# Values as two scaled f16 parts instead of three bf16 parts in the attention product of a fused attention and MLP kernel

## The chip, the cores and the metric

The kernel runs on 1 core of one Trainium2 chip. The metric is device microseconds of one execution, the median of several runs. Three runs of the kernel before gave 973.56, 976.33 and 977.08 us; the median is 976.33 us.

## The reference

Causal attention with a learned decay over 4 batches of 8 heads, 576 positions, head dimension 64, all in float32; then two MLPs with a squared ReLU, 2304 tokens, 512 features, 2048 hidden units.

```
scores = q @ k.T / 8 + (cum[i] - cum[j])     # cum = cumsum(log f), causal mask
attn   = softmax(scores)                     # rows
x      = attn @ v                            # (4, 8, 576, 64) -> (2304, 512)
h      = max(x @ w_in, 0);  x = (h * h) @ w_out
h      = max(x @ w_in2, 0); out = (h * h) @ w_out2
```

## The kernel before, in words

Every float32 product is taken apart into products of shorter parts, so that TensorE runs each at one pass. Nothing is issued in the order of the source: each piece of work is an `op` with an engine, an assumed duration, a priority, the ops it depends on and the buffers it uses. `Plan.run` walks a model of time over them and emits the instructions of every engine in the order it finds. That order is fixed in the program; on the chip each engine takes its instructions in order and waits on semaphores. When an op's assumed duration or its place among the buffers changes, the order of all engines changes with it.

The first 64 queries of every head (`first_part`) and the next 128 (`pair`) are done at the start, while the first MLP's weights are loaded, decoded and split. The remaining 384 queries of each head are a `unit(b, h)`: 32 units, eight to a batch. The first MLP (`mlp_a`, groups g = 0 to 8 of 256 tokens, products at L861 and L936, 12 matmuls to a block, 32 blocks to a group) fills TensorE between them. Group 3 needs all units of batch 0, group 4 those of batches 0 and 1. The second MLP (L1233, L1259) follows; its weights are prepared when the last unit is done.

A unit has these steps. SP loads q and k (`raw`, L652); ACT, DVE and POOL split them (L659 to L674). TensorE computes the scores in four pieces, two matmuls each (L713), into two banks `bk`. DVE takes the row maximum (L409), ACT the exponential (L417), DVE the reciprocal (L423, L426). ACT writes the high f16 part of the probabilities (`p_hi`, L432) and DVE the low one (`p_lo`, L439) into `ph`. SP issues a transposing DMA of `ph` into `pt` (L731). There is one `pt` buffer (`npt=1`), so the transpose of a unit is issued when the product of the unit before has read it. Then TensorE multiplies `pt` with the values (`av`, L750), and ACT (L766) and DVE (L768) add the upper and lower 64 rows of the result into `X` with the constant factor 2^-15.

The values of a head are loaded (L697) into every other row of 64 of a buffer `vv`, of which there are two. `v_parts` makes two subtractions on POOL (L448): the float32 numbers' upper halves serve as bf16 parts in place. In `av` the stationary operand of ten matmuls is 128 wide (high and middle part of the values beside each other), once for the high and once for the low part of the probabilities. Five more matmuls have the third part of the values, 64 wide, each put into one half of the output rows, as the table `THIRD` says.

Of the kernel before, what the change touches and what calls it, by code (L numbers as in the profile page):

```python
# [7 lines left out]
F32 = mybir.dt.float32  # L8
# [17 lines left out]
THIRD = ((0, 0), (1, 1), (3, 0), (2, 1), (4, 0))  # L26
# [39 lines left out]
class Op:  # L66
    __slots__ = ("how", "prio", "uses", "nwait", "ready", "outs", "data", "turn", "dmas", "rows")


class Plan:  # L70
# [17 lines left out]
    def op(self, eng, dur, fn, prio, deps=(), uses=(), data=None, other=None, dmas=1, rows=128):  # L88
# [3 lines left out]
        o.how, o.uses, o.data, o.dmas, o.rows, o.turn = {eng: (dur, fn, 0)}, tuple(uses), data, dmas, rows, dur == self.TURN[0]  # L92
# [13 lines left out]
    def run(self):  # L106
# [15 lines left out]
        while todo:  # L122
            again = True
            while again:
                again = False
                for e in engs:
# [66 lines left out]
                    if o.data is not None and e == "SP":  # L193
                        free[e] = t
                        _, a, z = self.TURN if o.turn else self.COPY
                        for _ in range(o.dmas):
# [4 lines left out]
                            end = lanes[issued % 8] = dma + self.LAT["DMA"] + (self.TURNED if o.turn else 0.0)  # L201
# [61 lines left out]
def attention_then_two_squared_relu_mlps(  # L263
# [111 lines left out]
    stat = ap_.tile([128, 2, 3, 8], F32, name="stat")  # L375
    PP = Pool([(x, stat[:, i, 0], stat[:, i, 1], stat[:, i, 2])
# [6 lines left out]
    ident = pair_p.tile([128, 128], F32, name="ident")  # L383
# [59 lines left out]
    def v_parts(vv, n, prio, dep):  # L443


        def rest(eng, i):
            x = vv()[:, :, i]
            eng.tensor_tensor(out=vv()[:, :, 1] if i == 0 else x.bitcast(BF16)[:, :, 0::2], in0=x,  # L448
                              in1=x.bitcast(BF16)[:, :, 1::2], op=ALU.subtract)

        for i in range(2):
            dep = either(TUNE["vr"], ("POOL", pool_(n * D), lambda i=i: rest(nc.gpsimd, i)),
                         ("DVE", dvs(n * D), lambda i=i: rest(nc.vector, i)), prio, [dep], [vv_of[vv]])
        return dep

    vv_of = {}
# [186 lines left out]
    def unit(b, h, prio, first):  # L643
# [5 lines left out]
        vv_of[vv] = vv  # L649
# [46 lines left out]
        def load_v():  # L696
            nc.sync.dma_start(out=vv()[:, :, 0], in_=v[b, h])  # L697

        ov = op("SP", P.COPY[0], load_v, prio + TUNE["vd"], [ld], [vv], data=0.91)
        ov = v_parts(vv, 5, prio + TUNE["vd"], ov)  # L700
# [35 lines left out]
        def av():  # L736
            x, w_, z = pT(), vv().bitcast(BF16), o()
# [787 lines left out]
```

## Time and profile before

| | |
|---|---|
| median of 3 runs | 976.33 us |
| the profiled execution | 977.94 us |
| its span, first to last instruction | 976.2 us |
| mean granted TensorE clock | 0.982 |
| TensorE busy | 948.3 us, 97% |
| VectorE (DVE), ScalarE (ACT), GpSimd (POOL) busy | 683.6, 453.1, 361.4 us |

The program is one core's, so there is one row of busy times. A busy TensorE at 97% says that whatever leaves its stream shortens the span, unless a wait takes its place; which waits are near is read stage by stage. The units lie between 131 us (first scores) and 484 us (last `av`).

### The profile page before, as it was taken

The page shows a single profiled execution, that of the slowest core. Times are in us where ns is not written, and L with a number is a line of the kernel's source. Part 1 is how long each engine was busy: PE and PEld are TensorE (multiplying, and loading weights), DVE is VectorE, ACT ScalarE, POOL GpSimd, SP SyncE. Part 2 cuts the span into 40 slices and gives each one's busy share as a digit, 9 for nine tenths or more (in the row PEclk, how much of TensorE's full clock was granted, in tenths as well). Part 3 has the DMA queues.
Part 4 walks back from the last instruction along what each step waited for, and adds up shares of the span by engine and source line. Part 5 has one row for each costly group of instructions (what it writes and reads, how often), then busy time and mean ns, then how long its engine had stood idle before and what let it go on. Part 6 is the DMA issues. An engine that isn't in the chain of part 4 may idle for free.

```text
span 976.2 us, 17134 instructions
## 1 busy us (share of the span) xinstructions
PE 948.3 (97%) x6463; PEld 866.7 (89%) x6463; DVE 683.6 (70%) x1341; ACT 453.1 (46%) x900; POOL 361.4 (37%) x315
## 2 busy tenths in 40 slices
PE   6999999999999999999999999999999999999997
PEld 3888898999997999999999998988898988989886
DVE  7998667787768778876478689888874445734343
ACT  3686677777777678775333353223230112311011
POOL 2244443444434435434232435332351314522130
PEclk7799999999999999999999999999999999999999
DMA  8767245666656756755546524674452111322113
GB/s 251 253 202 207 83 104 119 140 129 146 132 110 134 148 122 134 143 118 120 120 160 207 173 82 157 199 242 159 134 171 88 64 65 65 117 86 79 65 65 108
DMA packets 177187, 131.91 MB, mean 135 GB/s; under 512 B 140944, under 2 KB 155536, under 8 KB 175056
## 3 DMA queue, kind: packets, MB, share of 16 engines
q1 hardware_dynamic: 176848, 130.32, 49.1%
q8 instruction: 51, 0.84, 0.4%
q10 hardware_dynamic: 256, 0.49, 0.2%
q14 instruction: 32, 0.26, 0.1%
HBM read 85.07 MB, written 18.42 MB: 106 GB/s over the span
## 4 chain that ended last, share of the span: by engine, by line
PE 70%; DVE 11%; issue 9%; POOL 3%; ACT 3%; DMA 2%; POOLq 0%; SPq 0%; ACTq 0%; DVEq 0%
PE yp L936 16%; PE hp L861 16%; PE hp L1233 13%; PE bk L1259 10%; PE bk L750 5%; PE yp L1259 5%; PE bk L713 4%; POOL g L1246 2%; DVE ph L439 1%; DVE tmp L818 1%; DVE tmp L820 1%; DVE pp L409 1%; DVE w L1122 1%; POOL gt L886 1%; DVE w L837 1%
## 5 line engine op out<-in xcount | busy, mean ns | idle before, releaser
L936 PE MATMUL yp<-gt,w 128*128 128x256 f32 x1728 | 231.6, 283 | 1.8 <-POOL gt L886 1.7
L861 PE MATMUL hp<-xk,w 128*128 128x256 f32 x1728 | 227.7, 282 | 1.1 <-DVE w L837 0.8
L936 PEld LDWEIGHTS yp<-gt,w 128*128 128x128 f32 x1728 | 216.5, 189 | 6.2 <-POOL gt L886 3.1
L861 PEld LDWEIGHTS hp<-xk,w 128*128 128x128 f32 x1728 | 215.3, 190 | 3.0 <-DVE w L837 1.0
L886 POOL TENSOR_TENSOR gt<-sq,gt 128x512 fp32r<-128x512 f32 x72 | 97.3, 1352 | 154.4 <-ACT gt L883 135.9
L1259 PE MATMUL bk<-w,g 128*128 128x512 f32 x576 | 148.5, 394 | 0.7 <-POOL g L1246 0.7
L1246 POOL TENSOR_TENSOR g<-r,g 128x768 fp32r<-128x768 f32 x36 | 66.8, 1855 | 203.2 <-ACT g L1245 199.3
L1233 PE MATMUL hp<-w 128*128 128x384 f32 x630 | 123.9, 335 | 0.1
L1259 PEld LDWEIGHTS bk<-w,g 128*128 128x128 f32 x576 | 106.6, 188 | 18.7 <-POOL g L1246 1.6
L1245 ACT CAST g<-r 128x768 fp32r<-128x768 f32 x47 | 39.3, 835 | 180.1 <-DVE r L1244 180.0
L1233 PEld LDWEIGHTS hp<-w 128*128 128x128 f32 x630 | 111.7, 188 | 8.1 <-DVE st L1210 0.4
L417 ACT ACTIVATE pp<-pp,stat 128x448 f32<-128x448 f32 (+1 forms) x128 | 78.4, 613 | 44.6 <-DVE stat L409 37.0
L439 DVE SCALAR_TENSOR_TENSOR ph<-pp,stat,ph 128x320 f16<-128x320 f32 (+2 forms) x96 | 77.3, 814 | 15.5 <-ACT ph L432 13.9
L1210 DVE TENSOR_TENSOR r<-hp,st 128x384 f32<-128x384 f32 x62 | 34.5, 556 | 62.8 <-PE hp L1233 62.7
L448 POOL TENSOR_TENSOR vv<-vv 128x320 f32<-128x320 f32 x64 | 54.4, 850 | 54.8 <-DMA vv<-in_v_dram 42.1
L1244 DVE SCALAR_TENSOR_TENSOR r<-r 128x768 f32<-128x768 f32 x47 | 73.6, 1567 | 1.4
L1259 PE MATMUL yp<-w,g 128*128 128x512 f32 x288 | 74.5, 393 | 0.0
L1233 PE MATMUL hp<-w,far 128*128 128x384 f32 x378 | 74.1, 335 | 0.0
L870 ACT ACTIVATE sq<-hp 128x512 f32<-128x512 f32 x72 | 42.8, 594 | 66.8 <-PE hp L861 66.3
L1233 PEld LDWEIGHTS hp<-w,far 128*128 128x128 f32 x378 | 67.3, 188 | 4.7
L409 DVE CUSTOM_DVE_ANT_0 pp<-bk,mask 128x448 f32<-128x448 f32 (+1 forms) x128 | 59.4, 476 | 15.3 <-PE bk L713 9.9
L873 DVE SCALAR_TENSOR_TENSOR sq<-hp,sq 128x512 f32<-128x512 f32 x64 | 44.0, 688 | 35.1 <-ACT sq L870 34.7
(171 smaller groups left out, 1281.5 us busy)
## 6 DMA issues: line engine op xcount, KB each, us to landing
w<-wo_d SPq DMA_DIRECT2D x48, 512.0 KB
stage<-in_w_dram SPq DMA_DIRECT2D x26, 512.0 KB
raw<-in_qk_dram SPq DMA_DIRECT2D x32, 288.0 KB
wo_d<-part SPq DMA_DIRECT2D x16, 512.0 KB
ph<-in_w_dram SPq DMA_DIRECT2D x7, 1024.0 KB
st<-in_w_dram SPq DMA_DIRECT2D x6, 1024.0 KB
vv<-in_v_dram SPq DMA_DIRECT2D x32, 160.0 KB
qk_a<-in_qk_dram SPq DMA_DIRECT2D x16, 192.0 KB
```

Source lines behind the costliest of these rows:

```text
L409: nc.vector.tensor_tensor_reduce(out=x[:rows, c0:c0 + wd], in0=src, in1=msk, scale=-0.125, scalar=3.0e38 if first else nmax[:rows, 5:6], o ...
L417: nc.scalar.activation(out=x, in_=x, func=AF.Exp, scale=-1.0, bias=nmax[:rows, t:t + 1], accum_out=ssum[:rows, t:t + 1])
L439: nc.vector.scalar_tensor_tensor(out=flat[:rows, z:z + wd], in0=x, scalar=r, in1=flat[:rows, 128 * blk:128 * blk + wd], op0=ALU.mult, op1= ...
L448: eng.tensor_tensor(out=vv()[:, :, 1] if i == 0 else x.bitcast(BF16)[:, :, 0::2], in0=x, in1=x.bitcast(BF16)[:, :, 1::2], op=ALU.subtract)
L750: nc.tensor.matmul(dst.rearrange("p (n c) -> p n c", n=rh.shape[1]), lhsT=lt, rhs=rh, start=(i == 0), stop=(i == len(todo) - 1), skip_grou ...
L861: nc.tensor.matmul(ps, lhsT=lt, rhs=rh, start=(k_ == 0 and c == 0), stop=(k_ == KD - 1 and c == 2))
L886: eng.tensor_tensor(out=gt[1]()[:, :c], in0=sq()[:, :c], in1=f32(gt[0]()[:, :c]), op=ALU.subtract)
L936: nc.tensor.matmul(yp[d // 2]()[:, d % 2], lhsT=lt, rhs=rh, start=(i == 0 and c == 0 and d % 2 == 0), stop=(i == NF - 1 and c == 2), skip_ ...
L1233: nc.tensor.matmul(ps()[:, 0:TH], lhsT=lt, rhs=rh, start=(k_ == 0 and c == 0), stop=(k_ == 1 and c == 2))
L1244: o = op("DVE", dvs(TU), lambda r=r: nc.vector.scalar_tensor_tensor(out=r(), in0=r(), scalar=0.0, in1=r(), op0=ALU.max, op1=ALU.mult), e0, ...
L1246: l = either_vp(TU, lambda e, r=r, g=g: e.tensor_tensor(out=g()[:, 1], in0=r(), in1=f32(g()[:, 0]), op=ALU.subtract), e0, [h], [r, g])
L1259: nc.tensor.matmul(bank(ob[c]), lhsT=g()[:, a, c * 128:(c + 1) * 128], rhs=rw()[:, b], start=(p == 0 and x == 0 and z == 0), stop=(p == NP ...
```

## The change

The values of a head are scaled by a power of two, so that they fit f16, and split into two f16 parts: the high part by ACT (scaled copy), the low part by DVE (times the scale, minus the high part). The five 64-wide matmuls of `av` and the two subtractions on POOL are gone, and the values are loaded as one run of 320 numbers per partition. The fold takes the inverse scale from a table `up_down` instead of the constant.

The scale is one number for each head, from the largest absolute value of the head. A new function `scales(b)` loads all values of a batch once more, 2560 numbers per partition in pieces, heads spread over 16 partitions each; DVE reduces each piece to a maximum per partition. A float32 matmul with these maxima as a stationary operand and the identity as the moving one lays them along the columns of all 128 partitions; six small DVE instructions make the two factors for eight heads. For batch 0 the pieces (1024, 1024, 512) go into parts of `X` not yet in use, for the others five pieces of 512 go through the two halves of `st`. The third piece onward waits for the reduction of the piece two before.

```diff
-    def v_parts(vv, n, prio, dep):
-        def rest(eng, i):
-            x = vv()[:, :, i]
-            eng.tensor_tensor(out=vv()[:, :, 1] if i == 0 else x.bitcast(BF16)[:, :, 0::2], in0=x,
-                              in1=x.bitcast(BF16)[:, :, 1::2], op=ALU.subtract)
-        for i in range(2):
-            dep = either(TUNE["vr"], ("POOL", pool_(n * D), lambda i=i: rest(nc.gpsimd, i)),
-                         ("DVE", dvs(n * D), lambda i=i: rest(nc.vector, i)), prio, [dep], [vv_of[vv]])
+    def v_parts(vv, b, h, prio, dep):
+        up = up_down[:, b, 0, h:h + 1]
...
+        def hi():
+            nc.scalar.activation(out=parts_v(vv)[:, :, 0], in_=x(), func=AF.Copy, scale=up)
+        def lo():
+            nc.vector.scalar_tensor_tensor(out=parts_v(vv)[:, :, 1], in0=x(), scalar=up, in1=parts_v(vv)[:, :, 0], op0=ALU.mult, op1=ALU.subtract)
+        o = op("ACT", act(5 * D) + 0.09, hi, prio, [dep, scale_of[b]], [vv])
+        return op("DVE", dvs(5 * D) + 0.08, lo, prio, [o], [vv])
+    def scales(b, prio, pieces, deps):
+        src = v[b].rearrange("h (y q) n d -> (h y) (q n d)", y=128 // H)
...
+            o = op("SP", P.COPY[0], load, prio, deps + [os_[j - 2] if j > 1 else None], data=n * 0.00143, lag=2.0)
+            os_.append(op("DVE", dve(n), top_of, prio, [o]))
...
+        o = op("DVE", 0.08, lambda: nc.vector.tensor_reduce(out=top[:, 7:8], in_=top[:, 0:k], op=ALU.max, axis=mybir.AxisListType.X), prio, os_)
+        ps = Buf(BK)
+        def spread():
+            nc.tensor.matmul(ps()[:, 0:128], lhsT=top[:, 7:8].to_broadcast([128, 128]), rhs=ident, start=True, stop=True, skip_group_check=True)
+        o = op("PE", mm4(128), spread, prio, [o, o_m2], [ps])
...
+        for y in range(6):
+            o = op("DVE", 0.2 if y == 0 else 0.08, lambda y=y: step(y), prio, [o], [ps] if y == 0 else [])
+        scale_of[b] = o
...
-                    todo.append((z[:, q], w_[:, j].rearrange("p z d -> p (z d)")[:, 1::2], x[:, n.start + z0:n.stop + z0:n.step]))
-            for i, half in THIRD:
-                j, q, n = cuts[i]
-                todo.append((z[64 * half:64 * half + 64, q], w_[:, j, 1, 0::2], x[:, n]))
+                    todo.append((z[:, q], w_[:, j].rearrange("p z d -> p (z d)"), x[:, n.start + z0:n.stop + z0:n.step]))
...
-        o_av = op("PE", 1.65, av, prio, [o_tr, ov] + gone, [pT, vv, o])
+        o_av = op("PE", 1.35, av, prio, [o_tr, ov] + gone, [pT, vv, o])
...
+        scales(0, TUNE["BP0"] - 40.0, early, [decoded[14]] + aug_second)
+        scales(1, 3850.0, later, w_all + [all_att[-8]])
+        scales(2, 5350.0, later, w_all + [all_att[-8]])
+        scales(3, 6850.0, later, w_all + [all_att[-8]])
```

The change moves the order on every engine. In the changed program the lines below `v_parts` are higher by 55 to 61: scores are L771, `av` L805, the MLP products L916 and L991, the transpose L789, loads of q and k L710, of values L755 (of `scales` L479), the spread matmul L494, the high and low part of the values L458 and L461.

On TensorE, the end of the product of unit 15 (counted from 1), before, and what follows it; `64x384` and the like are the third parts:

```order
L750 LDWEIGHTS vv_103
L750 MATMUL bk_89<-pt_101,vv_103 128x128
L750 LDWEIGHTS vv_103
L750 MATMUL bk_89<-pt_101,vv_103 64x384
L750 LDWEIGHTS vv_103
L750 MATMUL bk_89<-pt_101,vv_103 64x384
L750 LDWEIGHTS vv_103
L750 MATMUL bk_89<-pt_101,vv_103 64x256
L750 LDWEIGHTS vv_103
L750 MATMUL bk_89<-pt_101,vv_103 64x384
L750 LDWEIGHTS vv_103
L750 MATMUL bk_89<-pt_101,vv_103 64x128
```

And the end of the same product now:

```order
L805 LDWEIGHTS vv_103
L805 MATMUL bk_89<-pt_101,vv_103 128x256
L805 LDWEIGHTS vv_103
L805 MATMUL bk_89<-pt_101,vv_103 128x128
L805 LDWEIGHTS vv_103
L805 MATMUL bk_89<-pt_101,vv_103 128x128
L991 MATMUL yp_93<-gt_81,w 128x256
```

The ten wide matmuls stay, the five narrow ones are gone, and an MLP block follows directly.

On TensorE, what stands between the products of units 15 and 16 before; in all there are three MLP blocks, and the eight score matmuls (L713) stand together:

```order
L861 MATMUL hp_92<-xk_83,w 128x256 x6
L713 MATMUL bk_87<-qk_1231 128x320
L713 MATMUL bk_87<-qk_1229 128x320
L713 MATMUL bk_88<-qk_1231 128x448
L713 MATMUL bk_88<-qk_1229 128x448
L713 MATMUL bk_87<-qk_1231 128x288
L713 MATMUL bk_87<-qk_1229 128x288
L713 MATMUL bk_88<-qk_1231 128x288
L713 MATMUL bk_88<-qk_1229 128x288
L936 MATMUL yp_94<-gt_81,w 128x256
```

And the same place now:

```order
L771 MATMUL bk_88<-qk_1237 128x320
L771 MATMUL bk_88<-qk_1235 128x320
L771 MATMUL bk_87<-qk_1237 128x448
L771 MATMUL bk_87<-qk_1235 128x448
L991 MATMUL yp_93<-gt_79,w 128x256
L991 MATMUL yp_93<-gt_80,w 128x256
L991 MATMUL yp_93<-gt_79,w 128x256 x2
L991 MATMUL yp_93<-gt_80,w 128x256
L991 MATMUL yp_93<-gt_79,w 128x256
L991 MATMUL yp_94<-gt_79,w 128x256
L991 MATMUL yp_94<-gt_80,w 128x256
L991 MATMUL yp_94<-gt_79,w 128x256 x2
```

An MLP block now follows the first four score matmuls, and there are five blocks between these two units. Between units 16 and 17 there are four now. Between most others there are five, as before.

On SP, the stretch from the transpose of unit 3 to that of unit 5 before (`pt<-ph` is a transpose, `raw` a load of q and k):

```order
L731 DMA_TRANSPOSE pt_101<-ph 128x26x128
L697 DMA vv_104<-in_v_dram 128x5x64
L652 DMA raw<-in_qk_dram 128x576
L731 DMA_TRANSPOSE pt_101<-ph 128x26x128
L697 DMA vv_103<-in_v_dram 128x5x64
L652 DMA raw<-in_qk_dram 128x576
L957 DMA y_d<-st 128x2x128 x4
L731 DMA_TRANSPOSE pt_101<-ph 128x26x128
```

And now:

```order
L789 DMA_TRANSPOSE pt_101<-ph 128x26x128
L755 DMA vv_104<-in_v_dram 128x320
L710 DMA raw<-in_qk_dram 128x576
L479 DMA st<-in_v_dram 128x512 x2
L789 DMA_TRANSPOSE pt_101<-ph 128x26x128
L755 DMA vv_103<-in_v_dram 128x320
L710 DMA raw<-in_qk_dram 128x576
L479 DMA st<-in_v_dram 128x512
L789 DMA_TRANSPOSE pt_101<-ph 128x26x128
L1012 DMA y_d<-st 128x2x128 x4
```

Loads of `scales` for the next batch (L479) now stand before two transposes in a row, and before the one ahead of them, too; the third to fifth of them wait for a reduction on DVE.

## Rows read from the trace of the kernel before

**Rows 1.** The page's first part: busy time, share and instructions of each engine.

```profile
PE 948.3 (97%) x6463; PEld 866.7 (89%) x6463; DVE 683.6 (70%) x1341; ACT 453.1 (46%) x900; POOL 361.4 (37%) x315
```

**Rows 2.** Windows: stretch, busy PE, PEld, DVE, ACT, POOL, then granted clock, DMA.

```profile
200.00:250.00 50.00, 49.72 (x401) 45.35 (x400) 37.99 (x109) 36.55 (x76) 19.38 (x20) 1.00 0.62 133
250.00:300.00 50.00, 49.55 (x401) 45.98 (x400) 36.61 (x104) 36.19 (x74) 20.96 (x21) 1.00 0.64 131
...
500.00:550.00 50.00, 50.00 (x425) 49.81 (x424) 39.53 (x53) 14.72 (x25) 17.11 (x13) 1.00 0.71 230
```

**Rows 3.** Timeline of TensorE, one `av` product, from its first, ninth, tenth, eleventh matmul.

```profile
181.92 1.93 PE L750 MATMUL bk<-pt,vv 128*128 128x384 f16 x15
...
183.12 0.56 PE L750 MATMUL bk<-pt,vv 128*128 128x128 f16 x4
...
183.18 0.50 PE L750 MATMUL bk<-pt,vv 128*128 128x128 f16 x3
...
183.33 0.52 PE L750 MATMUL bk<-pt,vv 128*64 128x384 f16 x5
183.78 0.40 PE L713 MATMUL bk<-qk 128*128 128x288 f32 x1
```

**Rows 4.** Timeline of TensorE from the end of one product to the next.

```profile
195.36 0.80 PE L713 MATMUL bk<-qk 128*128 128x288 f32 x4
...
202.36 1.53 PE L936 MATMUL yp<-gt,w 128*128 128x256 f32 x12
203.73 1.93 PE L750 MATMUL bk<-pt,vv 128*128 128x384 f16 x15
```

**Rows 5.** Lines by form, whole span: busy, mean ns, idle before, releasers.

```profile
L439 DVE SCALAR_TENSOR_TENSOR ph<-pp,stat,ph 128x320 f16<-128x320 f32 x32 | 24.3, 759 | 3.1 <-ACT ph L432 1.8
L432 ACT ACTIVATE ph<-pp,stat 128x320 f16<-128x320 f32 x32 | 17.7, 554 | 2.5 <-DMA pt<-ph 1.1 <-DVE stat L426 0.7 <-DVE stat L423 0.5
L448 POOL TENSOR_TENSOR vv<-vv 128x320 bf16<-128x320 f32 x32 | 28.9, 903 | 1.9
L448 POOL TENSOR_TENSOR vv<-vv 128x320 f32<-128x320 f32 x32 | 25.5, 796 | 53.0 <-DMA vv<-in_v_dram 42.1 <-PE bk L713 10.0 <-PE hp L861 0.7
L495 DVE TENSOR_REDUCE tmp<-tmp 128x8 f32<-128x512 f32 x2 | 1.4, 677 | 0.0
L426 DVE RECIPROCAL stat<-stat 128x1 f32<-128x1 f32 (+1 forms) x112 | 18.0, 161 | 2.7
```

**Rows 6.** Source L439: minimum, median, maximum ns, first and last start.

```profile
L439 DVE SCALAR_TENSOR_TENSOR ph<-pp,stat,ph x96: 534/789/1527, 134.3 to 471.7; 128x320 f16<-128x320 f32 x32, 128x448 f16<-128x448 f32 x32, 128x576 f16<-128x576 f32 x32
```

**Rows 7.** Timeline of TensorE, float32 transposes with the identity and what follows.

```profile
97.65 0.79 PE L615 MATMUL bk<-ident,pp 128*128 128x128 f32 x3 [0.53 <-ACT pp L605]
98.27 0.94 PE L589 MATMUL bk<-qk_a 66*128 66x192 f32 x6
```

**Rows 8.** Timeline of TensorE at units 15 and 16, and windows of the same stretch.

```profile
305.64 0.87 PE L713 MATMUL bk<-qk 128*128 128x320 f32 x4
307.92 1.08 PE L713 MATMUL bk<-qk 128*128 128x288 f32 x4 [1.41 <-DVE stat L409]
...
309.58 2.18 PE L936 MATMUL yp<-gt,w 128*128 128x256 f32 x11 [0.46 <-POOL gt L886]
311.56 2.96 PE L750 MATMUL bk<-pt,vv 128*128 128x384 f16 x15
314.46 1.68 PE L936 MATMUL yp<-gt,w 128*128 128x256 f32 x12
...
310.00:315.00 5.00, 5.00 (x29) 3.54 (x28) 4.09 (x9) 1.98 (x5) 2.69 (x3) 0.66 0.21 59
```

**Rows 9.** Timeline of SP: the transpose ahead of the product at 203.73.

```profile
195.47 4.01 SPq L731 DMA_TRANSPOSE pt<-ph  x1
```

**Rows 10.** Windows of the stretch in which batch 0's scales fall.

```profile
110.00:120.00 10.00, 9.08 (x73) 8.48 (x72) 3.56 (x4) 4.37 (x9) 5.97 (x12) 1.00 0.01 2
```

More of the change, by code (lines that the diff above doesn't have):

```diff
@@ L200, in run @@
                             dma = max(dma, dge + z) + o.data / o.dmas
-                            end = lanes[issued % 8] = dma + self.LAT["DMA"] + (self.TURNED if o.turn else 0.0)
+                            end = lanes[issued % 8] = dma + self.LAT["DMA"] + (self.TURNED if o.turn else 0.0) + o.lag
                             issued += 1
@@ L375, in attention_then_two_squared_relu_mlps @@
     stat = ap_.tile([128, 2, 3, 8], F32, name="stat")
+    top = ap_.tile([128, 8], F32, name="top")
+    ident = ap_.tile([128, 128], F32, name="ident")
+    up_down = ap_.tile([128, B, 2, H], F32, name="up_down")
     PP = Pool([(x, stat[:, i, 0], stat[:, i, 1], stat[:, i, 2])
@@ new lines, in attention_then_two_squared_relu_mlps, with load, top_of, step @@
+    scale_of = {}
+    def scales(b, prio, pieces, deps):
+        src = v[b].rearrange("h (y q) n d -> (h y) (q n d)", y=128 // H)
+        c, os_, last = 0, [], [None] * len(pieces)
+        for j, x in enumerate(pieces):
+            n = 1
+            for y in x.shape[1:]:
+                n *= y
+            def load(x=x, c=c, n=n):
+                s_ = src[:, c:c + n]
+                nc.sync.dma_start(out=x, in_=s_.rearrange("p (a c) -> p a c", a=x.shape[1]) if len(x.shape) == 3 else s_)
+            def top_of(x=x, j=j):
+                nc.vector.tensor_reduce(out=top[:, j:j + 1], in_=x, op=ALU.max, axis=mybir.AxisListType.XY if len(x.shape) == 3 else mybir.AxisListType.X,
+                                        apply_absolute_value=True)
+            o = op("SP", P.COPY[0], load, prio, deps + [os_[j - 2] if j > 1 else None], data=n * 0.00143, lag=2.0)
+            os_.append(op("DVE", dve(n), top_of, prio, [o]))
+            c += n
+        assert c == src.shape[1]
+        k = len(pieces)
+        o = op("DVE", 0.08, lambda: nc.vector.tensor_reduce(out=top[:, 7:8], in_=top[:, 0:k], op=ALU.max, axis=mybir.AxisListType.X), prio, os_)
[3 more added lines that the diff above has]
+        o = op("PE", mm4(128), spread, prio, [o, o_m2], [ps])
+        m, up, down = up_down[:, b, 1], up_down[:, b, 0].bitcast(U32), up_down[:, b, 1].bitcast(U32)
+        def step(y):
+            if y == 0:
+                nc.vector.tensor_reduce(out=m, in_=ps()[:, 0:128].rearrange("p (h y) -> p h y", h=H), op=ALU.max, axis=mybir.AxisListType.X)
+            elif y == 1:
+                nc.vector.tensor_scalar(out=m, in0=m, scalar1=1.0e-27, scalar2=None, op0=ALU.max)
+            elif y == 2:
+                nc.vector.tensor_scalar(out=down, in0=down, scalar1=0x7F800000, scalar2=None, op0=ALU.bitwise_and)
+            elif y == 3:
+                nc.vector.tensor_scalar(out=up, in0=down, scalar1=0x7F800000, scalar2=None, op0=ALU.bitwise_xor)
+            elif y == 4:
+                nc.vector.tensor_scalar(out=up_down[:, b, 0], in0=up_down[:, b, 0], scalar1=2.0 ** 13, scalar2=None, op0=ALU.mult)
+            else:
+                nc.vector.tensor_scalar(out=m, in0=m, scalar1=2.0 ** -29, scalar2=None, op0=ALU.mult)
+        for y in range(6):
+            o = op("DVE", 0.2 if y == 0 else 0.08, lambda y=y: step(y), prio, [o], [ps] if y == 0 else [])
+        scale_of[b] = o
@@ L736, in av @@
         def av():
[L737 removed]
+            x, w_, z = pT(), parts_v(vv), o()
             cuts = []
@@ L1423, in attention_then_two_squared_relu_mlps @@
         opened = op("POOL", 0.01, open_qk, TUNE["BP0"] - 1.0, a_tr + [o_ph])
+        early = [X[:, :, 768:1024], X[:, :, 0:256], X[:, 0:2, 768:1024]]
+        later = [st_[j % 2][:, 512:1024] for j in range(5)]
+        scales(0, TUNE["BP0"] - 40.0, early, [decoded[14]] + aug_second)
         for h in range(H):
```

25 lines of the change are left out of this document (13 added, 12 removed).

## The prediction

> **What bounds the kernel now.** I read the busy times first: TensorE is busy for 97% of the span [rows 1], so the time is what stands in its stream plus its waits. Then the windows by stage: through the units TensorE is busy for 49.7 and 49.6 of 50 us, and after the last unit for 50.00 of 50 [rows 2]. DVE (38.0 and 36.6 of 50) and ACT (36.6 and 36.2) are the engines with the least to spare beside it; POOL has more than half free. So what leaves TensorE's stream among the units is worth its full length, as long as DVE, ACT and the transposes keep up with a stream that arrives sooner. Third, the timeline of one product, for what its narrow matmuls cost; last, the one place among the units where TensorE does stand and loses clock [rows 8].
>
> **What goes from TensorE.** One product of 15 matmuls begins at 181.92 and the next work at 183.78: 1.86 us [rows 3]. The five narrow ones begin at 183.33 and hold the stream until 183.78, 0.45 us. There is more: the ninth matmul, of 128 columns, is followed by the tenth after 0.06 us, and the tenth, of the same 128 columns, by the first narrow one only after 0.15 us. So the step from 128-wide to 64-wide costs 0.09 us. Another such step leads back out; entering the product costs none, since the 12 matmuls before it, of another type and length, take 203.73 - 202.36 = 1.37 us, 0.114 each, with no gap left over [rows 4]. Without narrow matmuls the ten end 0.06 us after 183.18, that is at 183.24, and the next work starts there rather than at 183.78: 0.54 us. If the gap on leaving had another cause and stayed, it would be 0.45. 32 x 0.54 = 17.3 us; lower end 32 x 0.45 = 14.4. I take 17.3, since the gap on entering the narrow form is in the row and the change of type alone shows none.
>
> The Trainium skill (TensorEngine Tiling (Array Packing), Tiling Modes, Key Properties) says that changing the tiling mode, not just the tile, drains the engine. The trace agrees on the way in, 0.15 against 0.06 us. By the rule the gap on leaving goes as well and the sum is 17.3 us; if that gap belongs to the change to float32 work, it is 14.4, which is rival (a).
>
> **What is added to TensorE.** Four spread matmuls, float32, 128 columns. The nearest are the float32 transposes with the same identity: three take 98.27 - 97.65 = 0.62 us, 0.21 each [rows 7]. 4 x 0.21 = 0.8 us. They are work that was not there, so they cannot gain; if each stood for its DVE input as long as the longest such wait here, 1.41 us [rows 8], they would cost 6.5.
>
> **What is added to ACT.** One scaled copy of 128x320 to f16 per unit, 0.554 us as in the same form of `p_hi` [rows 5], 17.7 us in all, in place of POOL's work. A unit takes 8.37 us from product to product [rows 4] and 1.86 in it, 10.2; at 36.4 of 50 us ACT has 7.4 us of work in that. The new figure is 8.0 of 9.7 (8.37 and 1.32), 82%. It is hidden by TensorE's blocks as long as the order gives it room. New is that this copy waits for a DMA: POOL waited 42.1 us for the values over 32 loads, 1.3 us each [rows 5], and nobody minded. If ACT comes as early as POOL did, the exponentials queued behind it come 1.3 us later. I take 0, for the planner puts the copy where it expects the values to have landed, and POOL's early arrival was idleness; the upper end, 1.3 us on ACT in each unit, reaches TensorE as far as rival (b) counts it.
>
> **What is added to DVE, and taken off it.** The low part is the form of `p_lo` at 320: 0.759 us on average, 0.534 at least [rows 5, 6]. Per batch, `scales` reduces 2560 columns, five times 512 at 0.677 [rows 5], 3.4 us, and seven small instructions at 0.161, 1.1 us: 4.5 per batch, 0.56 per unit. What comes back: the spread from 534 to 1527 ns [rows 6] is mostly DVE standing beside POOL, whose two subtractions of 0.80 and 0.90 us per unit [rows 5] go. I take back 0.759 - 0.534 = 0.22 us per unit. Now 7.6 us per unit; then 7.6 + 0.76 + 0.56 - 0.22 = 8.7 of 9.7 us, 90%. That is the tightest engine, and TensorE's order was laid out with lower durations for it. A wait of TensorE for DVE was rare before; I charge half a microsecond at 8 places, two in a batch: 4 us. Bounds: none, or 0.5 us in each unit, 16.
>
> The Trainium skill (SBUF — State Buffer, SBUF: two separate sides) says that a DVE instruction with two inputs in SBUF and a GpSimd instruction lock each other out of one pair of ports. It speaks for the relief, and against the change too: the new low part has two such inputs and may stand behind POOL's remaining work. The rows agree in that the same kind of instruction takes 0.534 us or up to 1.527; by the rule the low part could cost DVE 1.527 - 0.759 = 0.77 us more in a unit than I count, at the most.
>
> **The transposes.** There is one `pt`, so a transpose starts when the product before has ended, and the next product needs it. In one cycle the product ends at 195.36, the transpose is issued at 195.47, and the next product begins at 203.73 without a wait [rows 4, 9]: it lands within 8.26 us. Five MLP blocks and the scores fill those 8.37 us before and now. SP has loads of `scales` ahead of nine transposes, in three batches. The issue of a transpose holds SP for 4.01 of these 10 us [rows 9], so the loads fit between unless they wait for DVE. I take 0 on average and keep the price for the last rival.
>
> **The place at units 15 and 16.** Before, only three blocks stood between these products: TensorE waited 1.41 + 0.46 us, then ran part of the time at the lower clock, 1.2 GHz (0.66 granted in the window), so that the product took 314.46 - 311.56 = 2.90 instead of 1.86 and the eleven matmuls before it 1.98 instead of 1.30 [rows 8]. That is 1.87 + 1.04 + 0.68 = 3.6 us. Now there are five blocks there, but four between units 16 and 17. Four blocks and scores are 8.37 less one block of 1.4, some 6.9 us against the 8.26 of a transpose, so 1.3 us of waiting may come back, with or without the clock. I take -2, bounds -3.6 and +1.
>
> **The start.** The loads and reductions for batch 0 fall where DMA stands still (0.01) and DVE has 3.56 of 10 us of work [rows 10]. Two reductions of 1024 stand ahead of the last weight's split, and the third load waits for the first reduction, so the spread may come late. I charge 1 us (0 to 3).
>
> **The sum.** -17.3 + 0.8 + 4 - 2 + 1 = -13.5 us. The profiled execution took 977.94 us (its span is 976.2, with 1.7 around it): 964.4. It was 1.6 above the median of the runs, 976.33, so I predict 963 us. The second MLP is unchanged, TensorE is full there, and the last unit ends sooner with more MLP blocks behind it, so nothing gives the time back later.
>
> **Rivals.** (a) Only the narrow matmuls go and the gap on leaving stays: 2.9 us less, about 966. For it: the gap on leaving is measured only toward float32 work. (b) DVE, at 90%, becomes the pace of the units: 0.5 us of waiting in each, 16 us, and the kernel stands at 975 to 977. For it: the one wait before was for DVE's maximum. Against: DVE's order was followed without waits for whole windows at 37 to 38 of 50. (c) No new waits and none at unit 16: -17.3 + 0.8 - 3.6 = -20, about 956. (d) Slower: a late transpose stops TensorE, and each stop takes clock with it, 3.6 us as in [rows 8]. With loads of `scales` ahead of nine transposes and the short stretch at unit 16 there are ten such places; from five stops on the gain of 16.5 is gone, at eight the time is 976 + 29 - 16.5 = 988. For it: before, TensorE had one such stop with fewer things on SP. Against: more than half of SP's time is free.
>
> **How the numbers follow.** Forecast 56%, its own range 959 to 969; (a) 12%, (b) 12%, (c) 10%, (d) 10%. The range that holds 8 in 10 takes in (a), most of (b) and (c): 956 to 977. Half a per cent, 4.9 us, is about what a measurement of this kernel can tell from no change. Faster by more than that (under 971.4): the forecast but for 2, (a) but for 1, (c), 75%; within: most of (b) and what is left of the two, 14%; slower: (d) and the end of (b), 11%.
>
> **What would show it.** In the profile after, L805 has 320 matmuls and a product takes about 1.32 us to the next work; the spread's four are near 0.2 us each; DVE is busy 43 to 45 of 50 us among the units; TensorE's waits there stay under 10 us and its clock at 1.00 but near unit 16. I am wrong if the product takes 1.41 (then a), if waits for DVE's maximum recur in each unit (b), or if the granted clock falls at several places behind transposes (d).

## The result, and the profile after

The changed kernel takes 980.16 us (median of five runs, 979.81 to 981.5), the kernel before, run beside it, 973.87: a ratio of 1.0059, 95% interval 1.0045 to 1.0072. It is 5.7 us slower by the ratio (6.3 between the medians), where I had predicted 963 us with 956 to 977 as the range. TensorE's part of the prediction is in the profile; what stood beside it is not where I put it.

The first part of the page after (busy us, share of the span of 979.6 us, instructions), which answers to [rows 1]:

```profile
PE 935.1 (95%) x6309; PEld 860.4 (88%) x6311; DVE 715.7 (73%) x1426; ACT 469.8 (48%) x927; POOL 307.4 (31%) x249
```

TensorE has 13.2 us less to do and the span is 3.4 us longer, so it stands still 16.6 us more. The windows (columns as in [rows 2]) say where most of it is:

```profile
200.00:250.00 50.00, 47.73 (x375) 44.48 (x375) 41.59 (x116) 41.54 (x85) 14.63 (x12) 1.00 0.65 137
250.00:300.00 50.00, 48.55 (x382) 45.05 (x381) 45.07 (x126) 39.66 (x81) 12.28 (x11) 1.00 0.75 160
500.00:550.00 50.00, 49.90 (x422) 49.53 (x421) 42.64 (x59) 17.16 (x29) 16.04 (x12) 1.00 0.68 224
```

Among the units TensorE is down from 49.7 and 49.6 of 50 us to 47.7 and 48.6; after them it is full. The granted clock is 1.00. Some of the standing lies ahead of the units: in the first 130 us TensorE is busy for 108.7 us instead of 113.3, and 2.4 of these 4.6 us fall between 30 and 60 us, long before the first load of the scales (103.4 us).

One `av` product on the timeline of TensorE (columns as in [rows 3]):

```profile
195.98 0.83 PE L771 MATMUL bk<-qk 68*128 68x320 f32 x3 [1.06 <-DVE qk L732]
196.65 1.58 PE L991 MATMUL yp<-gt,w 128*128 128x256 f32 x12
198.13 0.54 PE L771 MATMUL bk<-qk 128*128 128x288 f32 x2
198.51 1.48 PE L805 MATMUL bk<-pt,vv 128*128 128x384 f16 x10
199.80 0.52 PE L771 MATMUL bk<-qk 128*128 128x288 f32 x2
```

The product begins at 198.51 and the next work at 199.80: 1.29 us, where it was 1.86 [rows 3]. 31 of the 32 products take as long. That is 0.57 x 32 = 18 us, near the 17.3 predicted. The first row is the new thing: a score product (the second of its pair, 68 rows) waits 1.06 us for DVE's copy of q. All score products as one group, before (L713) and after (L771): busy us, mean ns, idle of TensorE just before them, and who ended it:

```profile
L713 PE MATMUL bk<-qk 68*128 68x288 f32 (+5 forms) x256 | 56.2, 326 | 3.6 <-DVE stat L409 2.3 <-DMA qk<-aug_d 1.2
```

```profile
L771 PE MATMUL bk<-qk 68*128 68x288 f32 (+5 forms) x256 | 63.1, 338 | 15.5 <-DVE qk L732 5.8 <-DMA qk<-aug_d 5.0 <-DVE stat L410 2.4
```

There are 15.5 us of idle time instead of 3.6, and TensorE is busy with the group for 6.9 us more. Single products are only 12 ns longer on average, 3 us over 256. The rest I put down to overlap, which the busy time counts once: above, twelve MLP products stand in 1.58 us, and a product that starts after a pause has none beside it. Together that is 18.8 us, so what the shorter product saves is lost again at the score products. Three inputs come late: DVE's copy of q (5.8 us), the load from `aug_d` (5.0), which ACT's queue issues, and DVE's maximum (2.4).

Why the copy was late at 195.98 stands on DVE's timeline after, in the six microseconds before:

```profile
189.60 0.85 DVE L823 SCALAR_TENSOR_TENSOR X<-bk,up_down,X 64x256 f32<-64x256 f32 x2 [0.21 <-ACT X L821]
190.47 0.15 DVE L424 TENSOR_SCALAR stat<-stat 128x1 f32<-128x1 f32 x1
190.54 0.45 DVE L410 CUSTOM_DVE_ANT_0 pp<-bk,mask 128x288 f32<-128x288 f32 x1
...
191.10 1.67 DVE L723 TENSOR_TENSOR qk<-raw,qk 64x576 fp32r<-64x576 f32 x1
192.69 0.68 DVE L1007 COPY st<-yp 128x512 f32<-128x512 f32 x1
193.40 0.52 DVE L410 CUSTOM_DVE_ANT_0 pp<-bk,mask,stat 128x288 f32<-128x288 f32 x1
...
193.84 0.68 DVE L482 TENSOR_REDUCE top<-st 128x1 f32<-128x512 f32 x1
194.56 0.16 DVE L490 TENSOR_REDUCE top<-top 128x1 f32<-128x5 f32 x1
...
194.93 0.68 DVE L440 SCALAR_TENSOR_TENSOR ph<-pp,stat,ph 128x448 f16<-128x448 f32 x1
...
195.60 0.33 DVE L732 CAST qk<-qk 64x384 fp32r<-64x384 f32 x1
```

DVE works without a pause for six microseconds and the copy (L732) is the last in its queue. Two of the rows ahead are reductions of the scales (L482, L490), and the low part of k (L723) takes 1.67 us instead of a usual 0.75. At that moment GpSimd has this instruction on its own timeline:

```profile
190.85 1.30 POOL L968 TENSOR_TENSOR xk<-X,xk 128x512 fp32r<-128x512 f32 x1 [2.27 <-ACT xk L964]
```

It ends at 192.15, and L723 began at 191.10: 1.05 us, about what L723 took too long. The durations of the new and changed steps after, by form (columns as in [rows 5]):

```profile
L461 DVE SCALAR_TENSOR_TENSOR vv<-vv,up_down 128x320 f16<-128x320 f32 x32 | 22.3, 698 | 2.8 <-ACT vv L458 2.0
L440 DVE SCALAR_TENSOR_TENSOR ph<-pp,stat,ph 128x320 f16<-128x320 f32 x32 | 18.2, 567 | 1.9 <-ACT ph L433 1.4
L458 ACT ACTIVATE vv<-vv,up_down 128x320 f16<-128x320 f32 x32 | 17.7, 554 | 0.4 <-DMA vv<-in_v_dram 0.2
...
L823 DVE SCALAR_TENSOR_TENSOR X<-bk,up_down,X 64x384 f32<-64x384 f32 x16 | 9.7, 607 | 0.6 <-ACT X L821 0.4
L821 ACT ACTIVATE X<-bk,up_down 64x384 f32<-64x384 f32 x16 | 9.2, 578 | 1.5 <-PE bk L805 0.9
...
L821 ACT ACTIVATE X<-bk,up_down 64x128 f32<-64x128 f32 x16 | 5.7, 358 | 3.4 <-PE bk L805 3.3
```

The folds of the kernel before, which I had left out of the prediction:

```profile
L768 DVE SCALAR_TENSOR_TENSOR X<-bk,X 64x384 f32<-64x384 f32 x16 | 8.8, 550 | 8.4 <-ACT X L766 8.3
L766 ACT ACTIVATE X<-bk 64x384 f32<-64x384 f32 x16 | 7.8, 488 | 5.7 <-PE bk L750 5.3
...
L766 ACT ACTIVATE X<-bk 64x128 f32<-64x128 f32 x16 | 4.3, 267 | 6.8 <-PE bk L750 6.7
```

### The profile page after: what moved, and what is told of

Read it like the earlier page. It is cut to its first block, busy times and chain, and to the rows that moved or that the text cites. A ratio compares the mean times of both kernels' runs of the same rounds, so it can differ in the third digit from the quotient of the medians.

```text
span 979.6 us, 16879 instructions
## 1 busy us (share of the span) xinstructions
PE 935.1 (95%) x6309; PEld 860.4 (88%) x6311; DVE 715.7 (73%) x1426; ACT 469.8 (48%) x927; POOL 307.4 (31%) x249
## 4 chain that ended last, share of the span: by engine, by line
PE 32%; issue 8%; DVE 7%; DMA 3%; POOL 3%; ACT 1%; POOLq 0%; SPq 0%; ACTq 0%; DVEq 0%
PE hp L1288 13%; PE bk L1314 10%; PE yp L1314 5%; DMA stage<-in_w_dram 3%; POOL g L1301 2%; PE hp L916 2%; PE yp L991 2%; DVE w L1177 1%; DVE lw L1128 1%; DVE X L1157 1%; DVE word L1128 1%; DVE sq L928 1%; DVE word L1126 0%; DVE part L1142 0%; PE bk L805 0%
## 5 line engine op out<-in xcount | busy, mean ns | idle before, releaser
L991 PE MATMUL yp<-gt,w 128*128 128x256 f32 x1728 | 232.0, 282 | 1.7 <-POOL gt L941 1.4
L916 PE MATMUL hp<-xk,w 128*128 128x256 f32 x1728 | 229.0, 282 | 2.6 <-POOL xk L968 1.5
L991 PEld LDWEIGHTS yp<-gt,w 128*128 128x128 f32 x1728 | 217.5, 189 | 4.1 <-POOL gt L941 3.6
L916 PEld LDWEIGHTS hp<-xk,w 128*128 128x128 f32 x1728 | 216.1, 190 | 4.1 <-POOL xk L968 1.7
L1301 POOL TENSOR_TENSOR g<-r,g 128x768 fp32r<-128x768 f32 x32 | 59.3, 1852 | 215.9 <-ACT g L1300 215.9
L771 PE MATMUL bk<-qk 68*128 68x288 f32 (+5 forms) x256 | 63.1, 338 | 15.5 <-DVE qk L732 5.8
L440 DVE SCALAR_TENSOR_TENSOR ph<-pp,stat,ph 128x320 f16<-128x320 f32 (+2 forms) x96 | 68.1, 714 | 8.7 <-ACT ph L433 7.7
L433 ACT ACTIVATE ph<-pp,stat 128x320 f16<-128x320 f32 (+2 forms) x96 | 62.8, 664 | 20.2 <-DVE stat L427 15.1
L1299 DVE SCALAR_TENSOR_TENSOR r<-r 128x768 f32<-128x768 f32 x47 | 71.4, 1520 | 1.4
L726 POOL TENSOR_TENSOR qk<-raw,qk 64x384 fp32r<-64x384 f32 x32 | 35.4, 1107 | 105.5 <-ACT qk L717 89.3
```

The costliest lines, as they stand in the source:

```text
L433: nc.scalar.activation(out=a, in_=x, func=AF.Copy, scale=r)
L440: nc.vector.scalar_tensor_tensor(out=flat[:rows, z:z + wd], in0=x, scalar=r, in1=flat[:rows, 128 * blk:128 * blk + wd], op0=ALU.mult, op1= ...
L771: nc.tensor.matmul(bk()[:, 0:c1 - c0], lhsT=x()[:rows, q0 - QA:wd - QA], rhs=x()[:rows, NQ + c0:NQ + c1], start=(y == 0), stop=(y == 1), s ...
L916: nc.tensor.matmul(ps, lhsT=lt, rhs=rh, start=(k_ == 0 and c == 0), stop=(k_ == KD - 1 and c == 2))
L991: nc.tensor.matmul(yp[d // 2]()[:, d % 2], lhsT=lt, rhs=rh, start=(i == 0 and c == 0 and d % 2 == 0), stop=(i == NF - 1 and c == 2), skip_ ...
L1299: o = op("DVE", dvs(TU), lambda r=r: nc.vector.scalar_tensor_tensor(out=r(), in0=r(), scalar=0.0, in1=r(), op0=ALU.max, op1=ALU.mult), e0, ...
```

## The experiments

Below each expectation stand the median, its ratio to the kernel before, run beside it (medians 973.86 to 975.56 us), and a 95% interval. Theory A: the work added to DVE and ACT makes the inputs of the score products late. Theory B: the scales alone do. Theory C: the units can't come faster whatever TensorE does. Theory D: what decides is the order that the planner lays, which comes out anew with every change of the work.

One thing has to be known first: the planner lays more than the order. Where a step may go to either of two engines (`either` in the source), it picks the engine too, and picks anew in each new plan. The copy of k in a unit is such a step. Before and after, its share on DVE:

```profile
L671 DVE CAST qk<-qk 64x576 fp32r<-64x576 f32 x8 | 5.1, 637 | 0.2
```

```profile
L729 DVE CAST qk<-qk 64x576 fp32r<-64x576 f32 x13 | 7.0, 540 | 0.4
```

Of the 32 copies DVE has 8 before, 13 in the changed kernel, and in e1 20, e2 8, e3 5, e4 4, e5 5, e6 22, e7 10, e8 7, e9 5, e10 4, e11 8, e12 7; ACT has the others. A few steps of the MLPs and of the weights change engines as well. Only e13 to e18 hold both the order and the engines (e16 those of the changed kernel, the others those of the kernel before).

**Parts taken away, each with a plan of its own**

e1, factors from a table laid once, no scales:

```diff
     def scales(b, prio, pieces, deps):
+        scale_of[b] = o_s15
+        return
...
+            nc.gpsimd.memset(up_down[:, :, 0], 2.0 ** 15)
+            nc.gpsimd.memset(up_down[:, :, 1], 2.0 ** -30)
```

> The changed kernel with constant factors (2^15 and 2^-30, laid once by GpSimd) in the table; the loads, reductions, spreading products and small steps that compute the factors are left out, the splits and the folds still read the table. Theory A (the split of v in each unit, 0.55 us on ScalarE and 0.70 us on VectorE, makes the parts of q and k and the maxima late for the score products; about 17 us of waits and stretched pairs): only the scales' own cost goes (spread 0.6 us, late start about 3 us), 975 to 977.5 us, waits ahead of the score products stay above 10 us. Theory B (the scales' loads, reductions of 1024 elements and chains of small steps cause the waits): 962 to 967 us, waits ahead of the score products back at some 4 us.

976.34 us, 1.0017 (1.0 to 1.0034), Theory A's figure: 3.8 us come back, and 13.5 us of idle time stay ahead of the score products.

e2, the scales added to the kernel before: its own code, with `scales` and its four calls.

> The kernel before, whole, with the computation of the scales added (loads, reductions, spread, small steps) and its result used by nobody. Theory A: about the start's delay and the spread, 3 to 5 us more than before: 976.5 to 979 us. Theory B: the waits come with it, 17 us and more: 985 to 993 us.

986.04 us, 1.0111 (1.0089 to 1.0133), Theory B's figure. But the score products wait only 5.2 us in it, so the 12 us are not the waits that B spoke of.

e3, the narrow products gone from the kernel before (the values' third piece is then incomplete):

```diff
-            for i, half in THIRD:
-                j, q, n = cuts[i]
-                todo.append((z[64 * half:64 * half + 64, q], w_[:, j, 1, 0::2], x[:, n]))
...
-        o_av = op("PE", 1.65, av, prio, ...
+        o_av = op("PE", 1.35, av, prio, ...
```

> The kernel before with the five narrow products of each head left out (a part of the value's third piece is then missing from the result), its split of v left on GpSimd. This is the gain on TensorE alone. Theory A: VectorE and ScalarE carry no more than before, so most of the 19 us is kept: 955 to 960 us. Theory B says the same. Theory C (the units cannot come faster than about 10.2 us each whatever TensorE does, since VectorE, ScalarE or the loads are already as fast as they go): 966 to 974 us, with new waits of 8 us and more ahead of the score products.

968.88 us, 0.9936 (0.9912 to 0.9959). TensorE's saving alone, with nothing put on DVE or ACT, brings 5 us and not 18: Theory C's outcome. The score products of this run:

```profile
L713 PE MATMUL bk<-qk 68*128 68x288 f32 (+5 forms) x256 | 59.5, 333 | 8.6 <-DVE qk L674 2.4 <-DVE stat L409 2.3 <-DMA qk<-aug_d 2.1
```

e4, as e1 with the low part on GpSimd and no factor for the high one:

```diff
-            nc.vector.scalar_tensor_tensor(out=parts_v(vv)[:, :, 1], in0=x(), scalar=up, ...
+            nc.gpsimd.tensor_tensor(out=parts_v(vv)[:, :, 1], in0=x(), in1=parts_v(vv)[:, :, 0], op=ALU.subtract)
```

> As the first kernel (no computed scales), and the low part of v is taken by GpSimd instead of VectorE, as x minus its f16 high part, unscaled (a constant factor 2^-15 in the folds). Theory A: VectorE gets 22 us back over the units, and the waits ahead of the score products fall to 4 to 7 us: 960 to 966 us, 10 us or more below the first kernel. Theory B: the same as the first kernel, 962 to 967 us both. Theory C: 966 to 974 us.

972.63 us, 0.9975 (0.9957 to 0.9993), Theory C's figure: 3.7 us below e1, where A said 10 or more. But DVE has 16 copies of k fewer in it than in e1, so the two don't differ by the low part alone. So far each theory has had its run.

e5, as e4 with the high part on GpSimd too and constants in the folds:

```diff
-            nc.scalar.activation(out=parts_v(vv)[:, :, 0], in_=x(), func=AF.Copy, scale=1.0)
+            nc.gpsimd.tensor_copy(out=parts_v(vv)[:, :, 0], in_=x())
```

> The changed kernel with both parts of v taken by GpSimd, unscaled (high part as a copy to f16, low part as the difference), factors constant as in the kernel before (2^-15 in the folds) and no scales: ScalarE and VectorE then do what they did before the change, and TensorE's av product is the shorter one, with nothing left out of the result. If the runs so far add up (narrow products gone -5, ScalarE's high part and the dearer folds about +4, VectorE's low part +4, scales +4), this stands where the kernel without narrow products stood: 967 to 970 us. If the high part on ScalarE and the folds cost nothing, it stays at the 972.6 us of the kernel with the low part on GpSimd.

965.94 us, 0.9902 (0.9883 to 0.9921), a little better than expected. It beats both kernels, though without scales it relies on values that f16 holds as they are.

e6, as e3 without the low parts of the probabilities:

```diff
-            p_ops.append(op("DVE", dvs(wd) + 0.06, lambda a=a: p_lo(*a), prio, [oh], [pp, ph]))
+            p_ops.append(oh)
```

> The kernel before without the five narrow products (as in the third run) and also without the low parts of the probabilities (77 us of VectorE, 2.1 us of every unit; they stay zero from the start, so the result lacks them); TensorE's work is that of the third run. Theory A in its wide form (VectorE's queue paces the units, so TensorE's saving can't be kept): the waits ahead of the score products fall under 4 us and the rest of the saving appears, 956 to 962 us. Theory C with another pace (ScalarE, the loads or the order in which they were laid): 965 to 970 us as in the third run.

964.27 us, 0.9892 (0.9874 to 0.9909). Between the two theories: some 5 us come. But DVE's busy time falls by 51 us (681.7 in e3, 630.7 here) and not by 77, since the planner gives it other steps, 17 more copies of k among them. So the run speaks against DVE's queue as the one pace, but not as clearly as planned. Score products then wait for `aug_d`, and an `av` product for its transpose, once 2.2 us.

**The same work planned anew**

e7 and e11 lay the kernel before, e8 the changed one, with longer assumed durations for the units' and first MLP's steps (30% of the way from the planner's figure to the trace's; e11 15%); e8 has nearly measured ones for the new steps too, e9 those alone, e10 the longer old ones alone. The expectation of e7 says that nothing but the order can differ; the choice of engines differs too. The edits, in effect, for instance:

```diff
-        o_k = op("ACT", act(S), k_hi, prio, [ld, opened], [ta, raw])
+        o_k = op("ACT", act(S) + 0.03, k_hi, prio, [ld, opened], [ta, raw])
...
-        return op("DVE", dvs(5 * D) + 0.08, lo, prio, [o], [vv])
+        return op("DVE", dvs(5 * D) + 0.22, lo, prio, [o], [vv])
```

> The kernel before, with the same instructions, laid out by the planner with longer assumed durations for the units' and the first MLP's steps on ScalarE, VectorE and GpSimd (30% of the way from what it assumes to what the trace shows); nothing but the order can differ. Theory D (the order laid with the old durations was picked on the chip for this kernel, and any other order is dearer): 977 to 985 us. If truer durations lay a better order: 968 to 973 us.

984.25 us, 1.01 (1.0083 to 1.0117): Theory D.

> The changed kernel with the same longer assumed durations, and with nearly the measured ones for the new steps (0.57 us for the high part, 0.69 us for the low part, 0.35 to 0.45 us for the scales' small steps). Theory D: the changed kernel's order was never picked for it, so another order may well be better: 970 to 977 us, and the waits ahead of the score products turn into MLP blocks. Theory A (VectorE's and ScalarE's work itself is too much, in any order): 978 to 985 us.

968.92 us, 0.9942 (0.9924 to 0.9959): below Theory D's own range, and below the kernel before.

> The changed kernel with its old assumed durations, except for the new steps, which get nearly the measured ones (high part 0.55, low part 0.70 us, reductions 0.1 us more, small steps 0.3 to 0.45 us). If the changed kernel lost its gain because the planner took the new steps for too short: 967 to 973 us, about as the replanned one (968.9). If any other order does as well or as badly: 970 to 983 us, and it need not be near the replanned one.

972.29 us, 0.9977 (0.9964 to 0.999), which both cases allow.

> The changed kernel with the longer assumed durations for the old steps alone (30% of the way to the trace) and the new steps as the change has them. If the new steps' short durations were the cause: it stays at 977 to 983 us. If it is the order as such (each order with its own waits, none of them picked for this kernel): 966 to 978 us, nearer the replanned 968.9 than the 980.2.

967.69 us, 0.9924 (0.9911 to 0.9936): the whole change with the new steps as short as before, and the best that it reached. So the short figures alone don't make the loss; the plan as a whole does. The score products still wait 11.6 us in it, against 15.5, and are busy for 61.1 us against 63.1: about half of its 12.5 us lies elsewhere.

> The kernel before, all its instructions, laid with assumed durations 15% of the way to the trace: a third order of the same work. If the order of the kernel before is a picked one (Theory D): 977 to 987 us again, with 8 to 12 us of waits ahead of the score products against its own 3.6. If the second order was merely a bad one: 970 to 977 us.

983.97 us, 1.0092 (1.0075 to 1.0108), but with 5.7 us of waits ahead of the score products, not 8 to 12: its loss is at other places too, the second MLP's among them. The score products of e7 and of e8:

```profile
L733 PE MATMUL bk<-qk 68*128 68x288 f32 (+5 forms) x256 | 60.1, 337 | 10.3 <-DMA qk<-aug_d 6.1 <-DVE qk L694 2.5 <-DVE stat L429 1.3
```

```profile
L791 PE MATMUL bk<-qk 68*128 68x288 f32 (+5 forms) x256 | 60.5, 342 | 7.8 <-DMA qk<-aug_d 3.8 <-DVE stat L430 2.3 <-DVE qk L752 1.5
```

So the plan of the kernel before is the best of its three by 9 us, and the plan of the changed kernel the worst of its four by 8 to 12.5. The few waits of the kernel before belong to its plan: e7 does the same work and has 10.3 us. How much of this is the order and how much the choice of engines, no run separates. It also means that e1 to e6, each with its own plan, can't be added up.

e12, e5 with the longer old durations:

> The kernel with both parts of v split by GpSimd and no scales (965.9 us), laid with the longer assumed durations for the old steps (30% of the way to the trace). If these lay a better order whenever the order was not picked: 958 to 963 us, less than both kernels and than the same split in the old order. If an order is a matter of chance: 964 to 975 us.

967.43 us, 0.9928 (0.9915 to 0.9941), no better than e5. Longer assumed durations don't lay a better plan as such.

**Work and order crossed**

e13 to e15, e17 and e18 keep the order of the kernel before, and its engines, to the instruction (in e15 a pair of score products and one reciprocal stand a little later): the planner gets its old figures (1.65 us for the product, two GpSimd steps in place of the split), the new steps have no length for it and are issued as soon as they can.

```diff
-        o = op("ACT", act(5 * D) + 0.09, hi, prio, [dep, scale_of[b]], [vv])
-        return op("DVE", dvs(5 * D) + 0.08, lo, prio, [o], [vv])
+        o = op("ACT", 0.0, hi, prio, [dep, scale_of[b]], [vv])
+        o = op("DVE", 0.0, lo, prio, [o], [vv])
+        for i in range(2):
+            dep = op("POOL", pool_(5 * D), lambda: None, prio, [dep], [vv])
+        return op("POOL", 0.0, lambda: None, prio, [dep, o])
```

e13, ten products, both parts on GpSimd, no scales:

> No narrow products, both parts of v split by GpSimd (as in the fifth run), but laid with the assumed durations of the kernel before, so that TensorE, VectorE, ScalarE and SyncE run exactly the order of the kernel before. If its order is what keeps waits low: TensorE's 19 us come nearly whole, 955 to 960 us, waits ahead of the score products 4 to 8 us. If the other engines pace the units in that order: 964 to 970 us, with the saving turned into waits ahead of the score products.

966.43 us, 0.9911 (0.9893 to 0.9928). The other engines pace the units: some 9 us come, not 19.

e18, the high part on ACT:

> The thirteenth run (split by GpSimd, in the order of the kernel before, 966.4 us) with the high part on ScalarE (0.55 us a unit) and the low part left on GpSimd, constants in the folds. If VectorE's low part (0.70 us a unit) is what makes the scores late: 965 to 970 us, and the rest up to the run before this one is the low part's. If ScalarE's part costs as much: 972 to 978 us.

970.79 us, 0.9965 (0.9951 to 0.9979), between its two cases.

e17, the low part on DVE as well, ACT's with a factor from the table, constants in the folds:

> The fourteenth run (split by ScalarE and VectorE, in the order of the kernel before, 984.0 us) with constants in the folds in place of the table (ScalarE's and VectorE's folds some 0.09 and 0.06 us shorter each, 7 us over the units on both engines). If the folds' scale is a part of the 17.6 us: 976 to 981 us. If it is the split alone: 982 to 986 us.

976.85 us, 1.0032 (1.0019 to 1.0045): the folds are part of the cost.

e14, the folds with the table's factors:

> Constant factors, the split as in the change (high part by ScalarE, low part by VectorE, folds with the table), laid into the order of the kernel before: all its instructions in its order, the new ones inserted as each load lands. The prediction's step (the split lies beside TensorE's work): within 2 us of the run with the split on GpSimd in the same order. Theory A (the split makes the scores late): 6 to 16 us above that run.

983.98 us, 1.0088 (1.0071 to 1.0104): 17.6 us above e13. The prediction's step fails, Theory A's figure is exceeded.

e15, the scales as well:

> The whole change, scales too, laid into the order of the kernel before. The prediction's sum with the order left alone: 960 to 966 us. Theory A (work on VectorE and ScalarE, in any order): 975 to 985 us, about what the changed kernel shows.

1008.77 us, 1.035 (1.0325 to 1.0375), far above both. The score products of e13, e18, e17, e14 and e15, in this order:

```profile
L774 PE MATMUL bk<-qk 68*128 68x288 f32 (+5 forms) x256 | 59.0, 332 | 7.5 <-DVE stat L410 4.2 <-DMA qk<-aug_d 2.3 <-DVE qk L735 0.8
```

```profile
L775 PE MATMUL bk<-qk 68*128 68x288 f32 (+5 forms) x256 | 60.7, 335 | 10.0 <-DVE stat L410 4.5 <-DMA qk<-aug_d 3.0 <-DVE qk L736 1.6
```

```profile
L777 PE MATMUL bk<-qk 68*128 68x288 f32 (+5 forms) x256 | 61.6, 337 | 12.1 <-DVE stat L410 4.9 <-DMA qk<-aug_d 2.8 <-DVE qk L738 2.3
```

```profile
L777 PE MATMUL bk<-qk 68*128 68x288 f32 (+5 forms) x256 | 62.3, 338 | 17.8 <-DVE stat L410 5.7 <-DVE qk L738 4.8 <-DMA qk<-aug_d 3.3
```

```profile
L774 PE MATMUL bk<-qk 68*128 68x288 f32 (+5 forms) x256 | 62.7, 344 | 26.9 <-DVE stat L410 18.2 <-DVE qk L735 4.8 <-DMA qk<-aug_d 1.6
```

Read the idle column down: 7.5, 10.0, 12.1, 17.8, 26.9 us, with DVE's maximum (L410) the chief releaser; next come the load from `aug_d` in the first three and DVE's copy of q in the last two. With the order held, each piece of work put on ACT and DVE shows in the time: 4.4 us for the high part, 6.1 for the low part (with ACT's dearer factor), 7.1 for the folds, 24.8 for the scales. The kernel before ran 1.4 us faster beside e17 and e18 than beside the others; by the ratios the four are 5.3, 6.5, 5.5 and 25.5 us. The last holds the poor place that the scales get there, ahead of everything; no run gave them a better place in this order. The split's place has a part as well: ahead of the low part DVE waits for ACT's high part, 8.3 us in e17 and 8.2 in e14, against 2.0 in the changed kernel. So what the work costs and what its place costs is not separated.

e16, all the work of the kernel before in the order of the changed kernel:

> All the work of the kernel before (three parts of v, 15 products), laid into the order of the changed kernel. Theory D (the changed kernel's order is a poor one in itself): 988 to 999 us, the 19 us of TensorE on top of the 980 us. Theory A (the waits come from VectorE's and ScalarE's added work, which is not there): 974 to 982 us.

986.77 us, 1.0121 (1.0099 to 1.0142), between the two theories. The four corners:

| us | order of before | order of after |
|---|---|---|
| work of before | 973.9 to 975.6 | 986.8 |
| work of after | 1008.8 | 980.2 |

Of the two plans, each work does best in the one laid for it. The new plan wins back 28.6 us of what the change costs in the old one. It leaves 5.7, and three other plans of the same work show that 8 to 12.5 us more were to be had.

## Why the prediction was wrong

**TensorE's saving: right as work, wrong as time.** I had 17.3 us and the product shows 18; rival (a) is out. But "what leaves TensorE's stream among the units is worth its full length" fails already without any added work: in the old order, e13 keeps some 9 us. TensorE arrives sooner at score products whose inputs don't come sooner: 7.5 us of idle time there against 3.6, and 2.8 us more of busy time.

**ACT and DVE: the step that failed.** The loads were sized well: DVE at 41.6 and 45.1 of 50 us (43 to 45 predicted), ACT's copy 554 ns as in [rows 5], with 0.4 us of waiting before it in all, the low part 698 against 759 ns, and the 320-wide `p_lo` down from 759 to 567 (a relief of 192 ns, where I took back 220; [rows 6], from which I read the spread, mixes three widths). What failed is "hidden by TensorE's blocks as long as the order gives it room", with ACT at 0 and DVE at 4 us. The score products' idle time rose by 11.9 us and their busy time by 6.9 in place of these 4. With order and engines held, the split on ACT and DVE alone costs 10.4 us (e13 to e17). I read the rarity of waits before as slack of the engines. It was a property of one plan: e7 and e11 do the same work in other plans and lose 9 us. Rival (b), to which I gave 12%, came nearest, in the place and in the size (16 us). But it named DVE's maximum, which ends 2.4 of the 15.5 us, and DVE as the pace, against which e6 speaks; ACT's late `aug_d` loads stand beside DVE's late copies.

**The folds: forgotten.** They read a factor from a table now, and I gave them no term. The rows show 90 and 91 ns more per ACT fold (578 against 488, 358 against 267) and 57 more per DVE fold of 384 (607 against 550); e17 and e14 differ by 7.1 us for it (5.5 by the ratios). The Trainium skill (ScalarE: Activation LUTs, What ACT_TABLE_LOAD costs) gives about 93 ns for each such pointer operand of an ACTIVATE, whatever its length; the rows agree at both lengths.

**The scales.** I had 0.161 us for each small step. Those of the first batch, on DVE and GpSimd:

```profile
117.56 0.17 DVE L503 TENSOR_SCALAR up_down<-up_down 128x8 f32<-128x8 f32 x1
117.77 0.99 DVE L505 TENSOR_SCALAR up_down<-up_down 128x8 uint32<-128x8 uint32 x1
118.79 1.19 DVE L507 TENSOR_SCALAR up_down<-up_down 128x8 uint32<-128x8 uint32 x1
120.02 1.21 DVE L509 TENSOR_SCALAR up_down<-up_down 128x8 f32<-128x8 f32 x1
```

```profile
117.69 1.04 POOL L932 TENSOR_TENSOR sq<-sq 128x512 f32<-128x512 f32 x1 [2.01 <-ACT sq L925]
118.69 1.27 POOL L968 TENSOR_TENSOR xk<-X,xk 128x512 fp32r<-128x512 f32 x1
119.91 1.28 POOL L941 TENSOR_TENSOR gt<-sq,gt 128x512 fp32r<-128x512 f32 x1
```

Three steps of eight columns last as long as the GpSimd instruction beside them and end with it. The Trainium skill (SBUF — State Buffer, SBUF: two separate sides) says that one of the two engines blocks until the other's instruction is over. I had cited it for two-input instructions; it names DVE instructions in a two-port mode as well, and here single-input ones show the wait (in which mode they ran, no row tells). The first score product of the units begins at 134.0 instead of 130.8 us: 3 us where I had 1, at the end of my bounds. In e1, without scales, it begins at 128.9 us. But that has its own plan, and 2.4 us of TensorE's standing are older than the scales, as said above; what the scales cost at the start stays open.

**The rest.** The four spread products hold TensorE's stream for 0.8 us by their start times, as predicted, and wait 0.8 us besides. No `av` product waited for its transpose, so rival (d) is out. The stop at units 15 and 16 is gone from the profile, as predicted. In its place TensorE stands 1.5 us between units 16 and 17, at a granted clock of 1.00, where I had 1.3 us. That the size fits is luck: I expected a late transpose there, and it waits for DVE's copy of q (0.99 us) and maximum.

**What stays open.** Why the changed kernel's own plan is the worst of four is not settled. Truer figures for the new steps alone (e9) brought 8 us, longer ones for the old steps alone (e10) 12.5, and for the kernel before the latter cost 9. So the planner's short figures for the new steps are not shown as the cause; a draw among plans that differ by 10 us explains it as well. An untested rival is the choice of engines: DVE has 13 copies of k in the changed kernel and 4 to 7 in its three better plans. A run with the changed kernel's order and those copies on ACT would tell.

## What to carry to other kernels

Where a planner lays the order, a change of the work is also a new plan, and here a new plan alone moved the time of the same work by 8 to 12.5 us, more than the change's effect: compare several plans of each version, or hold the plan and change the work. Check whether the planner also chose other engines. Few waits in a profile show that this plan fits this work; they don't show how much work the engines that TensorE waits for could still take. When a constant becomes a table entry, price every instruction that reads it.

## What the runs showed of the hardware

Besides the pointer operand and the blocked small steps above: in e13 GpSimd's copy of 128x320 to f16 took 521 ns and its subtraction 930, so both parts of v cost it 1.45 us a unit against 1.70 for the three parts [rows 5].
